# First feed-forward layer over two chunks at once: products of 256 columns in a Strassen-like scheme, with both chunks' state chains in one window

## The chip, the cores and the metric

The kernel runs on one core of a Trainium2 chip. The metric is the device time of one execution in microseconds (us). A core has a matrix engine (TensorE, PE in the profile, with its weight loads shown as PEld), three engines for elementwise work (VectorE = DVE, ScalarE = ACT, GpSimd = POOL) and SyncE (SP), whose queue issues nearly all DMAs here. Each engine works through its own instructions in order; semaphores tie the engines together. Matrix products accumulate in PSUM, everything else lives in SBUF, 128 partitions wide.

## What is computed

Two blocks in a row, all in float32: a delta-rule attention over 4 batches, 8 heads, 768 steps, head size 48, and a feed-forward net with an exact GELU on its 3072 tokens of 384 values (hidden size 2048).

```python
k_n = k / (np.linalg.norm(k, axis=-1, keepdims=True) + 1e-06)
state = np.zeros((B, H, D, D))
for t in range(S):
    kt, vt, bt = k_n[:, :, t], v[:, :, t], beta[:, :, t, None]
    y[:, :, t] = np.einsum('bhd,bhde->bhe', q[:, :, t], state)
    v_old = np.einsum('bhde,bhd->bhe', state, kt)
    state = state + bt[..., None] * np.einsum('bhd,bhe->bhde', kt, vt - v_old)
x = y.transpose(0, 2, 1, 3).reshape(B * S, H * D)
h = x @ w_in
out = (0.5 * h * (1.0 + erf(h / sqrt(2)))) @ w_out
```

The weights come as 64-bit floats and are decoded on the chip in the first part of the run.

## The kernel before

**Tiling.** The 768 steps are cut into 12 chunks of 64. A chunk has two tiles (`Unit`, u.a = 0, 1), each with two batches on the 128 partitions, so a chunk is 256 tokens for the feed-forward net. Two chunks make a group (32 tile-heads, four tiles).

**State chain of a chunk.** `against_state` multiplies the state by the keys and the queries (K products, L667, 64 matmuls); `subtract` forms W = (K product - V) times a factor on DVE (L678, L684) and copies y on ACT (L679); `solve` multiplies W by the group's inverse (L702), and ACT copies the result U (L710, L712); `use` forms the chunk's outputs and the state's increment (L732, L743); `next_state` (L748) and `read` (L758) add them on DVE; `turns` transposes the outputs x on PE (L788), and ACT copies them to xT. Only then the feed-forward net can begin on this chunk. The next chunk's chain needs the new state.

**What a group needs beforehand.** Keys and queries are loaded by DMA into block layouts (`load_blocks`, L138, eight DMAs a tile) and transposed on DVE (`turned_k` L399 into Kt, six buffers; `turned_q` L404 into Qt). `grams` (L414) multiplies keys by keys, `queries` (L414, then L450 on DVE) queries by keys, giving P. `norms` and `prep` square the keys on ACT, reduce on DVE (L349) and raise to a power on POOL (L351); `finish` (L303 to L307 on DVE) makes the factors; `scale_v` multiplies V by the norms on POOL (L376). The elimination (`eliminate_steps`) inverts 32 x 32 triangles on DVE, all of a group's at once: `scales` (L476, then the product of the mask `low` with the factors, L477, into XM), `flip` (a transpose, L482), `scaled_flip` (L487), 28 rows of two operations each (L501 writes tmp, L503 adds it to Nu) and two more L496, the diagonal L507, and transposes back into XM (L512) and Zf (L516). `join_run` then joins the 32 x 32 blocks to 64 x 64 (J1, J2: PE L593, DVE L605, ACT L572 into Zf).

**Feed-forward net.** Chunks 0 and 1 run it plainly (`fc1` L811, products of 256 columns; `fc2` L829, 384 columns). From chunk 2 on, both layers use a Strassen-like scheme with 7 instead of 8 products. In the first layer `mix_x` (L884) makes the input sums on DVE; then for each block of hidden features come eleven groups of matmuls in the order P1 P5 P6 P2 R22 R11 P7 P3 R12 P4 R21 (`part_of_layer`, L916). The two operands that the scheme combines are the chunk's two tiles, so a product has 128 columns. A chunk has NB = 2 blocks with FB = 4 matmuls in each group, 88 matmuls. DVE adds partial sums (L939 after P6, `add_p5` L968, L947 after P7, L958 after P4), and ACT copies and applies GELU into G (L902). P7, P4 and R21 add to the accumulator that L939 and L968 have worked on, P4 and R21 after L947 has read it. In the second layer `mix` makes the sums of G (L976, L977, L979, L981), seven products of eight matmuls with 192 columns follow (`second_layer`, L859), and `read2` (L1010 to L1021) puts the output together.

**Order.** A plan of (time, step) pairs is sorted and emitted; one unit of time is one chunk of the feed-forward net, and FFN(c) fills the unit from c+1 to c+2. DVE executes its steps exactly in the emitted order. PE runs in `together` blocks tied to the line of feed-forward products (`behind`). The chain of chunk c stands in FFN(c-1). The elimination of a group is given times from -0.35 to 1.167 around an odd unit (`rows_of`), so its rows lie over some one and a half units. So DVE has its rows, the sums of both layers and the chain's small operations in one order, and a step that waits holds up everything behind it on DVE.

Of the kernel before, what the change touches and what calls it, by code (L numbers as in the profile page):

```python
# [19 lines left out]
def kernel(  # L20
# [28 lines left out]
    nc = tc.nc  # L49
# [120 lines left out]
    low = cpool.tile([128, HB, HB], F32)  # L170
# [11 lines left out]
    G = cpool.tile([128, NA, NF, 128], F32)  # L182
# [126 lines left out]
    def squares(u, n, engine=None):  # L309
        kd = u.Kn[:, :, 0:D]  # L310
        if engine is nc.gpsimd:
            ksq = su.tile([128, H, D], F32, tag="w_e", name="ksq")
        else:
            ksq = wk.tile([128, H, D], F32, tag="x", name="ksq")
        if engine is None:
            keep(nc.scalar.activation, ksq, kd, ACT.Square)
            u.ksq = ksq
            return
        engine.tensor_tensor(ksq, kd, kd, op=ALU.mult)
        nc.vector.tensor_reduce(n, ksq, axis=AX.X, op=ALU.add)  # L320

    def sum_of_squares(u, h):

        if "both" not in ns:
            n23 = wk.tile([128, 2 * NA, H], F32, tag="n23", name="n23", bufs=1)
            ns[2], ns[3] = n23[:, 0:NA], n23[:, NA:]
            ns["both"] = n23
        if h == 0:
            u.ksq = wk.tile([128, H, D], F32, tag="ksq", name="ksq", bufs=1)
        keep(nc.scalar.activation, u.ksq[:, h], u.Kn[:, h, 0:D], ACT.Square,  # L330
             accum_out=ns[u.c][:, u.a, h:h + 1])
# [138 lines left out]
    def eliminate_steps(g):  # L470
        steps = []

        def scales():
# [3 lines left out]
            (nc.vector if g > 1 else nc.gpsimd).tensor_tensor(gl, low, gt.unsqueeze(2).to_broadcast([128, HB, HB]),  # L477
                                    op=ALU.mult)
# [172 lines left out]
    def against_state(us):  # L651

        for u in us:
            u.W = wk.tile([128, H, D], F32, tag="W", name="W")
# [53 lines left out]
    def solved(u, copy):  # L708
        u.U = wk.tile([128, H, D], F32, tag="U", name="U")
# [40 lines left out]
    def read(u, copy=nc.scalar.copy):  # L750
        u.x = wk.tile([128, H, D], F32, tag="x", name="x")
# [13 lines left out]

    def turn(u):
        if u.a == 0:
            xTs[u.c] = wk.tile([128, NM, NA * 128], F32, tag="xT", name="xT")
# [13 lines left out]
    def turns(us):  # L782
        c = us[0].c
        xT = xTs[c] = wk.tile([128, NM, NA * 128], F32, tag="xT", name="xT")
# [66 lines left out]
    A = [[G[:, a, k * FH:(k + 1) * FH] for k in range(2)] for a in range(NA)]  # L851
# [10 lines left out]
    FB = FH // 2  # L862
    NB = FH // FB
    S1, L1 = {}, {}

# [10 lines left out]
    def of_x(c, k, a):  # L876
        return xTs[c][:, k, a * 128:(a + 1) * 128]

    def mix_x(c):
        t = more[0].tile([128, 3, 128], F32, tag="TX", name="TX")  # L880
# [25 lines left out]
    def part_of_layer(c, b, n):  # L906

        fs = slice(b * FB, (b + 1) * FB)
# [11 lines left out]
        def half(k, a):  # L920
            return A[a][k][:, fs]

        def fresh(name, tag, pool):
            L1[name] = pool.tile([128, FB, 128], F32, tag=tag, name=f"ps{name}")
            return L1[name]

        if n == "P1":
            if b == 0:
                L1["pu"] = more[0].tile([128, 2, FB, 128], F32, tag="S1", name="pu")
# [12 lines left out]
        elif n == "R11":  # L942
            product(L1["X1"], block(0, 2), of_x(c, 2, 0), False)
            keep(nc.scalar.activation, half(0, 0), L1["X1"], ACT.Gelu)
        elif n == "P7":
            product(L1["Y1"], S1[3], L1["T"][3], False)
            nc.vector.tensor_tensor(half(1, 1), L1["Y1"], L1["pu"][:, 0], op=ALU.add)  # L947
# [8 lines left out]
        elif n == "P4":  # L956
            product(L1["Y1"], block(1, 1), L1["T"][4], False)
            nc.vector.tensor_tensor(half(0, 1), L1["V1"], L1["pu"][:, 1], op=ALU.add)  # L958
        else:
            product(L1["Y1"], block(1, 2), of_x(c, 2, 0), False)  # L960
            keep(nc.scalar.activation, half(1, 0), L1["Y1"], ACT.Gelu)
# [8 lines left out]
    def mix(c, n, h):  # L970
        fs = slice(h * FH // 2, (h + 1) * FH // 2)
        a11, a12, a21, a22 = (A[a][k][:, fs] for a in range(2) for k in range(2))
        if n == 1:
            if h == 0:
                W2["S"] = L1["pu"].rearrange("q e f n -> q (e f) n")
# [7 lines left out]
    def two(c, n):  # L983
        if n == 1:
# [56 lines left out]
    def ffn_steps(c):  # L1041
        ones = [(1.3, fc1, c, f) for f in range(NF)]
        if c > 1:
            return [(0.88, part_of_layer, c, b, n) for b in range(NB)
                    for n in ("P1", "P5", "P6", "P2", "R22", "R11", "P7", "P3", "R12", "P4", "R21")] + [
                (2.6, second_layer, c, n) for n in (1, 5, 2, 6, 4, 7, 3)]
# [131 lines left out]
    def late():  # L1178
# [3 lines left out]
        for a in range(NA):  # L1182
            Kb = more[0].tile([128, 2, NP, 2, HB], F32, name=f"Kb{a}")
            nc.scalar.mul(Kb.rearrange("q p j h n -> q (p j h n)"),
                          low.rearrange("q a b -> q (a b)")[:, 0:NP * 4 * HB], 0.0)
            for c in range(5, NC, 2):
                tiles[c, a].Kb = Kb
# [8 lines left out]
    plan = [at(c + 1 + 0.25 * (c == 1), c + 2 + 0.25 * (c == 0), ffn_steps(c)) for c in range(NC)]  # L1196
# [25 lines left out]
    plan += [at(c + 0.958, c + 0.959, [(1.0, mix_x, c)]) for c in range(2, NC)]  # L1222
    plan += [at(c - 0.4, c - 0.3, v_steps(c)) for c in range(4, NC)]
    plan += [at(2.08, 2.44, [(1.0, scale_head, tiles[c, a], h)
                             for c in (2, 3) for a in range(NA) for h in range(H)])]
    plan += [at(c - 1.0, c - 0.99, [(1.0, load_v, c)]) for c in range(3, NC)]
    for c in range(4, NC):
        us = [tiles[c, a] for a in range(NA)]
        t = {4: 1.8, 5: 2.1, 6: 3.25}.get(c, c - 2.9)
        plan += [at(t, t + 0.01, [(1.0, load_blocks, c, "Kb", k)])]  # L1230
        t = 3.2 if c == 4 else c - (0.72 if c % 2 == 0 else 0.9)
        plan += [at(t, t + 0.01, [(1.0, load_blocks, c, "Qb", q)])]
        t = c - (2.1 if c % 2 == 0 else 2.62) if c > 5 else {4: 2.1, 5: 2.74}[c]
        plan += [at(t, t + 0.01, [(1.0, load_k, c, "Kn")])]
        plan += [at(c - 0.4, c - 0.39, [(1.0, load_k, c, "Kp")])]
        t = {4: 2.7262, 5: 2.955}.get(c, c - (1.77 if c % 2 == 0 else 2.57))
        plan += [at(t, t + 0.0005, [(1.0, turned_k, u) for u in us])]
        t = c + (-0.12 if c % 2 == 0 else 0.23)
# [19 lines left out]
    for c in range(2, NC):  # L1258
        for b in range(NB):
            t = c + 1.06 + 0.2576 * b  # L1260
            plan += [at(t, t + 0.001, [(1.0, add_p5)])]
        plan += [at(c + 1.42, c + 1.421, [(1.0, mix, c, 1, 0)]),
                 at(c + 1.94, c + 1.941, [(1.0, read_x, c)]),
                 at(c + 1.715, c + 1.716, [(1.0, mix, c, 3, h) for h in range(2)])]
    for w in range(3, NC):
        two_ahead = w + 2 < NC
        if w % 2:
            if w == 3:
                plan += [at(w + 0.19, w + 0.191, [(1.0, transposed, u, (1,)) for u in fourth]),
                         at(w + 0.1, w + 0.101, [(1.0, together, *gram(5))]),  # L1270
                         at(w - 0.07, w - 0.069, [(1.0, norms, 5)]), at(w - 0.039, w - 0.038, [(1.0, prep, 5)]),
                         at(w + 0.11, w + 0.111, [(1.0, finish, 4)])]
                plan += rows_of(2, w, ((1, 0.112, 0.113), (2, 0.16, 0.2), (4, 0.224, 0.31),
                                       (2, 0.325, 0.365), (1, 0.395, 0.4), (2, 0.485, 0.5),
                                       (2, 0.508, 0.54), (5, 0.6, 0.685), (7, 0.76, 0.88),
                                       (3, 1.0, 1.05), (5, 1.07, 1.1), (1, 1.153, 1.154),
                                       (1, 1.2, 1.201), (1, 1.201, 1.202)))
            elif two_ahead:
                plan += rows_of(w // 2 + 1, w, ((1, -0.35, -0.349), (1, -0.34, -0.339),
                                                (1, -0.23, -0.229), (5, -0.22, -0.14),  # L1280
                                                (1, -0.07, -0.06), (3, 0.005, 0.05),
                                                (3, 0.068, 0.148), (2, 0.156, 0.215),
                                                (2, 0.235, 0.31), (3, 0.325, 0.365),
                                                (1, 0.398, 0.409), (2, 0.485, 0.5),
                                                (1, 0.508, 0.54), (5, 0.6, 0.685),
                                                (3, 0.76, 0.8), (1, 1.003, 1.004),
                                                (1, 1.16, 1.161), (1, 1.166, 1.167)))
            plan += [state_at(w, w + 0.367, w + 0.59, w + 0.72, w + 0.93, second=query(w))]
        else:
            j0, j1, j2 = join_steps(w // 2)  # L1290
            t = w + (0.25 if w == 4 else 0.165)
            plan += [at(t, t + 0.001, [(1.0, together, j0, *query(w))]),
                     at(w + 0.37, w + 0.371, [(1.0, together, j1, *gram(w + 2))]),
                     state_at(w, w + 0.465, w + 0.58, w + 0.72, w + 0.93, second=[j2] + gram(w + 3))]
            plan += spread("join", 4, w + 0.395)
            plan += spread("join", 4, w + 0.64)
            if two_ahead:
                plan += spread("gram", 2, w + 0.375) + spread("gram", 2, w + 0.42)
                plan += spread("gram", 4, w + 0.63)
                plan += [at(w + 0.366, w + 0.367, [(1.0, norms, w + 2)]), at(w + 0.3715, w + 0.372, [(1.0, prep, w + 2)]),  # L1300
                         at(w + 0.56, w + 0.561, [(1.0, norms, w + 3), (1.0, prep, w + 3)]),
# [33 lines left out]
```

## Time and profile before

| | |
|---|---|
| median of three runs | 640.89 us (640.38 to 640.94) |
| span of the profiled execution, first to last instruction | 638.7 us |
| mean granted TensorE clock | 0.985 |
| ACT busy | 259.9 us (41%) |
| POOL busy | 64.9 us (10%) |
| first-layer products, psX | 480 matmuls, 64.5 us |
| second-layer products, psX | 320 matmuls, 55.3 us |

Each float32 matmul is carried out in two recorded passes, and the recorded length of one holds its pipeline's tail: the pitch from one start to the next is what a matmul costs. By slices of a fortieth of the span (16 us), the digits are tenths of busy time; PEclk is the granted clock:

```profile
PE   6779999999999999999999999999999999999997
DVE  6999989999799987999677999577999565354342
POOL 4044002100300012001012001012001000000000
PEclk9977999999999999999999999999999999999999
```

After the first two or three slices PE has hardly any idle time. DVE alternates, and its last quarter is light, since no elimination is left. From 214 us on the chunks have a regular period of 45 to 46 us.

### The profile page before, as it was taken

How to read it: one execution, taken by the hardware profiler on the slowest of the kernel's cores; microseconds unless marked ns; L12 is line 12 of the kernel's file. 1: busy time of each engine (PE TensorE's matmuls, PEld its weight loads, DVE VectorE, ACT ScalarE, POOL GpSimd, SP SyncE). 2: the span in 40 equal slices, each digit the busy share in tenths (PEclk: the TensorE clock that was granted, in tenths of full speed). 3: DMA queues.
4: the chain of work that ended last, by engine and by line, in shares of the span. 5: the costliest groups of instructions: out<-in, count | busy, mean ns of one | idle time of the engine just before them, and what ended most of it. 6: DMA issues, size and time to landing. Idle time of an engine off the chain costs nothing.

```text
span 638.7 us, 22156 instructions
## 1 busy us (share of the span) xinstructions
PE 618.4 (97%) x9702; PEld 573.8 (90%) x9702; DVE 496.6 (78%) x1011; ACT 259.9 (41%) x586; POOL 64.9 (10%) x58
## 2 busy tenths in 40 slices
PE   6779999999999999999999999999999999999997
PEld 5667776776899999999999999999999999999997
DVE  6999989999799987999677999577999565354342
ACT  3576877624541265132265132265142253231230
POOL 4044002100300012001012001012001000000000
PEclk9977999999999999999999999999999999999999
DMA  9794884303442234221335222311222300100101
GB/s 134 172 280 139 149 175 137 50 1 73 73 67 44 47 51 77 56 36 36 58 48 79 54 27 47 57 27 28 52 29 38 62 4 2 26 2 3 26 2 25
DMA packets 158433, 39.79 MB, mean 62 GB/s; under 512 B 150016, under 2 KB 153216, under 8 KB 158336
## 3 DMA queue, kind: packets, MB, share of 16 engines
q1 hardware_dynamic: 155664, 37.34, 30.2%
q8 instruction: 76, 1.25, 0.8%
q10 hardware_dynamic: 2672, 1.03, 0.8%
q14 instruction: 21, 0.17, 0.1%
HBM read 33.62 MB, written 4.72 MB: 60 GB/s over the span
## 4 chain that ended last, share of the span: by engine, by line
PE 81%; DVE 11%; ACT 2%; DMA 2%; issue 2%; POOL 0%; SPq 0%; DVEq 0%; ACTq 0%; POOLq 0%
PE psX L859 12%; PE psY L916 11%; PE psX L916 8%; PE psY L859 8%; PE psV L916 5%; PE psZ L916 5%; PE psG L414 5%; PE psZ L859 4%; PE psV L859 4%; PE psK L667 3%; PE psO L829 3%; PE psJ L593 2%; DVE tmp L501 2%; DVE Nu L503 2%; PE psH L811 2%; PE psY L732 2%
## 5 line engine op out<-in xcount | busy, mean ns | idle before, releaser
L916 PE MATMUL psX<-xT,w_in_sb 128*128 128x128 f32 x480 | 64.5, 277 | 0.0
L503 DVE TENSOR_TENSOR Nu<-Nu,tmp 128x58 f32<-128x58 f32 (+13 forms) x168 | 58.5, 348 | 5.8
L501 DVE TENSOR_TENSOR tmp<-Nu 128x58 f32<-128x58 f32 (+13 forms) x168 | 59.2, 352 | 4.4
L916 PEld LDWEIGHTS psX<-xT,w_in_sb 128*128 128x128 f32 x480 | 58.8, 192 | 1.2 <-issue 0.3
L902 ACT COPY xT<-psX 128x768 f32<-128x768 f32 x9 | 7.2, 799 | 124.3 <-PE psX L788 124.3
L351 POOL TENSOR_TENSOR n<-n,half 128x16 f32<-128x16 f32 x10 | 30.2, 3020 | 247.2 <-DVE n L349 197.4
L859 PE MATMUL psX<-w_out_sb,G 128*128 128x192 f32 x320 | 55.3, 326 | 0.0
L859 PEld LDWEIGHTS psX<-w_out_sb,G 128*128 128x128 f32 x320 | 52.1, 190 | 0.0
L811 PE MATMUL psH<-xT,w_in_sb 128*128 128x256 f32 x192 | 44.4, 384 | 1.5 <-ACT G L902 1.3
L829 PE MATMUL psO<-w_out_sb,G 128*128 128x384 f32 x128 | 43.9, 490 | 0.0
L811 PEld LDWEIGHTS psH<-xT,w_in_sb 128*128 128x128 f32 x192 | 35.7, 190 | 8.8 <-ACT G L902 2.2
L916 PE MATMUL psY<-xT,w_in_sb 128*128 128x128 f32 x320 | 42.3, 275 | 0.0
L902 ACT COPY pu<-psZ 128x512 f32<-128x512 f32 x40 | 23.5, 587 | 39.5 <-PE psZ L916 39.5
L916 PEld LDWEIGHTS psY<-xT,w_in_sb 128*128 128x128 f32 x320 | 38.9, 192 | 0.0
L829 PEld LDWEIGHTS psO<-w_out_sb,G 128*128 128x128 f32 x128 | 23.6, 190 | 14.0
L902 ACT ACTIVATE G<-G 128x512 f32<-128x512 f32 x40 | 25.2, 629 | 20.5 <-DVE G L947 19.8
L376 POOL TENSOR_TENSOR V<-V,n 128x384 f32<-128x384 f32 x18 | 17.2, 965 | 135.3 <-DMA V<-in_v_dram 131.1
L939 DVE TENSOR_TENSOR psY<-psY,pu 128x512 f32<-128x512 f32 x20 | 14.0, 699 | 20.5 <-PE psY L916 18.7
L859 PE MATMUL psZ<-T,pu 128*128 128x192 f32 x160 | 28.6, 332 | 0.0
L859 PE MATMUL psY<-T,G 128*128 128x192 f32 x160 | 28.6, 332 | 0.0
L859 PE MATMUL psV<-w_out_sb,G 128*128 128x192 f32 x160 | 27.7, 326 | 0.0
L859 PE MATMUL psX<-T,G 128*128 128x192 f32 x160 | 27.6, 326 | 0.0
(183 smaller groups left out, 1349.7 us busy)
## 6 DMA issues: line engine op xcount, KB each, us to landing
Kp<-in_k_dram SPq DMA_DIRECT2D x76, 96.0 KB, 3.1
w_out_sb<-in_moe_w_in_dram SPq DMA_DIRECT2D x24, 256.0 KB, 4.1
w_raw<-in_moe_w_out_dram SPq DMA_DIRECT2D x16, 384.0 KB, 4.8
V<-in_v_dram SPq DMA_DIRECT2D x48, 96.0 KB, 3.1
out_dram<-o_sb SPq DMA_DIRECT2D x40, 96.0 KB, 2.2
Qp<-in_q_dram SPq DMA_DIRECT2D x64, 32.0 KB, 2.1
Qp<-in_q_dram SPq DMA_DIRECT2D x16, 96.0 KB, 4.4
Qp<-in_k_dram SPq DMA_DIRECT2D x32, 32.0 KB, 2.2
```

The lines of the kernel that those rows point to most:

```text
L351: nc.gpsimd.tensor_tensor(flat, flat, half, op=ALU.pow)
L376: engine.tensor_tensor(u.V, u.V, ns[u.c][:, u.a].unsqueeze(2).to_broadcast([128, H, D]), op=ALU.mult)
L414: nc.tensor.matmul(psG[HALF[p], r, i * NP + j, :], lhsT=u.Kt[rows, p, j, :], rhs=(u.Qt if x else u.Kt)[rows, p, j, :], start=True, stop=True)
L501: nc.vector.tensor_tensor(tmp, nu[:, j + 1:, j:j + 1].to_broadcast([128, n, j]), nu[:, j:j + 1, 0:j].to_broadcast([128, n, j]), op=ALU.mult)
L503: nc.vector.tensor_tensor(nu[:, j + 1:, 0:j], nu[:, j + 1:, 0:j], tmp, op=ALU.add)
L667: nc.tensor.matmul(u.psK[to, x, r, j, :], lhsT=(u.Qt if x else u.Kt)[rows, p, j, :], rhs=St[rows, u.a, p ^ r, j, :], start=True, stop=True)
L811: nc.tensor.matmul(psH, lhsT=w_in_sb[:, f // 2, m, f % 2 * 128:(f % 2 + 1) * 128], rhs=xTs[c][:, m, :], start=(m == 0), stop=(m == NM - 1))
L829: nc.tensor.matmul(u.psO, lhsT=G[:, u.a, f, :], rhs=w_out_sb[:, f, :], start=(f == 0), stop=(f == NF - 1))
L859: nc.tensor.matmul(ps_, lhsT=lhs[:, f, :], rhs=rhs[:, f, :], start=first and f == 0, stop=f == FH - 1, skip_group_check=not first)
L902: i = fn(*args, **kw)
L916: nc.tensor.matmul(ps_[:, i], lhsT=lhs[:, f // 2, f % 2 * 128:(f % 2 + 1) * 128], rhs=rhs, start=first and i == 0, stop=True, skip_group_c ...
L939: nc.vector.tensor_tensor(L1["Y1"], L1["Y1"], L1["pu"][:, 0], op=ALU.add)
```

## The change

From chunk 4 on the first layer runs over pairs of chunks (4,5), (6,7), (8,9), (10,11). The operands that the scheme combines are now the two whole chunks, so a product has 256 columns; a pair has four blocks with two matmuls in each group, 88 matmuls a pair. After a pair's first layer the second layers of both its chunks follow, unchanged. For that:

- G is there twice, xT holds a pair, and both state chains of a pair run in the window before: chunk 4's and 5's in FFN(3), chunk 6's and 7's in the second layers of pair (4,5), and so on.
- To make room, V, W, U and x of a tile share one buffer (a new V is loaded after `turns` has read x), `low` and the early squares live in the second G until it is used, the two extra tiles for odd chunks' key blocks are gone (all chunks use the same two), and the key squares use the tile of `mix_x`.
- From group 1 on XM is made by an `affine_select` on POOL instead of a product with `low` (on DVE for groups 2 to 5).
- All rows of the elimination for groups 3, 4, 5 stand in the first layer of the pair before, up to the join; group 2's stay where they were.
- Loads, transposes, norms and V's scaling get new times. Among them the transposes L399 for chunk 6 go from 4.23 to 3.5, into FFN(2), those for chunk 7 stay at 4.43, and those for later chunks go from c-1.77 and c-2.57 to c-2.5 and c-2.92.

```diff
@@ scales
-            (nc.vector if g > 1 else nc.gpsimd).tensor_tensor(gl, low, gt.unsqueeze(2).to_broadcast([128, HB, HB]),
-                                    op=ALU.mult)
+            wide = gt.unsqueeze(2).to_broadcast([128, HB, HB])
+            if g == 0:
+                nc.gpsimd.tensor_tensor(gl, low, wide, op=ALU.mult)
+            else:
+                nc.gpsimd.affine_select(out=gl, in_=wide, compare_op=ALU.is_ge, fill=0.0, base=-1,
+                                        pattern=[[1, HB], [-1, HB]], channel_multiplier=0)
@@ against_state, solved, read
-            u.W = wk.tile([128, H, D], F32, tag="W", name="W")
+            u.W = u.V
...
-        u.U = wk.tile([128, H, D], F32, tag="U", name="U")
+        u.U = u.W
...
-        u.x = wk.tile([128, H, D], F32, tag="x", name="x")
+        u.x = u.U if u.c else wk.tile([128, H, D], F32, tag="y", name="x")
@@ turns, of_g, blocks, of_x, part_of_layer
+    def new_tokens(c):
+        if c % 2 == 0:
+            xTs["pair", c] = wk.tile([128, NM, 2, NA * 128], F32, tag="xT", name="xT", bufs=1)
+        xTs[c] = xTs["pair", c - c % 2][:, :, c % 2]
...
+    def of_g(c):
+        g = Gp[c % 2 if c > 3 else 0]
+        return [[g[:, a, k * FH:(k + 1) * FH] for k in range(2)] for a in range(NA)]
...
+    def blocks(c):
+        return FH // 2 if c < 4 else FH // 4
...
     def of_x(c, k, a):
+        if c > 3:
+            return xTs[c + a][:, k]
         return xTs[c][:, k, a * 128:(a + 1) * 128]
...
+        FB = blocks(c)
+        NB = FH // FB
+        n_ = 512 // FB
...
-            L1[name] = pool.tile([128, FB, 128], F32, tag=tag, name=f"ps{name}")
+            L1[name] = pool.tile([128, FB, n_], F32, tag=tag, name=f"ps{name}")
@@ ffn_steps
-                (2.6, second_layer, c, n) for n in (1, 5, 2, 6, 4, 7, 3)]
+                (2.6, second_layer, cc, n) for cc in range(c, c + 1 + (c > 3))
+                for n in (1, 5, 2, 6, 4, 7, 3)]
@@ late
-        for a in range(NA):
-            Kb = more[0].tile([128, 2, NP, 2, HB], F32, name=f"Kb{a}")
...
-            for c in range(5, NC, 2):
-                tiles[c, a].Kb = Kb
@@ plan
-    plan += [at(c - 0.4, c - 0.3, v_steps(c)) for c in range(4, NC)]
+    plan += [at(t, t + 0.1, v_steps(c)) for c in range(4, NC)
+             for t in (4.3 if c == 5 else c - (0.4 if c % 2 == 0 else 0.85),)]
...
-        t = {4: 1.8, 5: 2.1, 6: 3.25}.get(c, c - 2.9)
-        plan += [at(t, t + 0.01, [(1.0, load_blocks, c, "Kb", k)])]
...
+        for name, src, t in (("Kb", k, {4: 1.8, 5: 2.73, 6: 3.25}.get(c, c - (2.8 if even else 3.45))),
+                             ("Qb", q, {4: 3.2, 5: 3.9}.get(c, c - (1.2 if even else 1.24)))):
+            plan += [at(t, t + 0.01, [(1.0, load_blocks, c, name, src)])]
...
-        t = {4: 2.7262, 5: 2.955}.get(c, c - (1.77 if c % 2 == 0 else 2.57))
+        t = {4: 2.7262, 5: 2.955, 7: 4.43}.get(c, c - (2.5 if even else 2.92))
         plan += [at(t, t + 0.0005, [(1.0, turned_k, u) for u in us])]
...
+    for w in range(4, NC, 2):
+        more_to_come = w + 2 < NC
+        if w == 4:
+            begins = 0.25, 0.33, 0.41, 0.51, 0.6, 0.66, 0.7, 0.78, 0.87, 0.945
+            n6, p6, n7, p7 = 0.53, 0.56, 0.75, 0.8
+        else:
+            begins = -0.22, -0.1, 0.02, 0.14, 0.27, 0.38, 0.42, 0.6, 0.76, 0.93
+            n6, p6, n7, p7 = 0.3, 0.34, 0.56, 0.58
+            plan += rows_of(w // 2, w, ((1, *((-1.19, -1.189) if w > 6 else (-1.05, -1.049))),
+                                        (1, *((-1.18, -1.179) if w > 6 else (-1.04, -1.039))),
+                                        (1, -1.035, -1.034), (4, -1.03, -1.0),
+                                        (3, -1.0, -0.95), (3, -0.935, -0.855), (2, -0.843, -0.785), (1, -0.77, -0.75),
+                                        (3, -0.742, -0.692), (3, -0.677, -0.597), (2, -0.585, -0.527), (1, -0.512, -0.5),
+                                        (3, -0.484, -0.434), (3, -0.419, -0.339), (2, -0.327, -0.269),
+                                        (2, -0.255, -0.245), (2, -0.24, -0.23)))
+        begins = [w + t for t in begins]
+        j0, j1, j2 = join_steps(w // 2)
+        plan += [at(begins[0], begins[0] + 0.001, [(1.0, together, j0, *query(w))]),
+                 at(begins[1], begins[1] + 0.001, [(1.0, together, j1, *gram(w + 2))]),
+                 state_at(w, *begins[2:6], second=[j2] + gram(w + 3)),
+                 state_at(w + 1, *begins[6:], second=query(w + 1))]
...
+            plan += [at(w + n6, w + n6 + 0.001, [(1.0, norms, w + 2)]), at(w + p6, w + p6 + 0.001, [(1.0, prep, w + 2)]),
+                     at(w + n7, w + n7 + 0.001, [(1.0, norms, w + 3)]), at(w + p7, w + p7 + 0.001, [(1.0, prep, w + 3)]),
+                     at(w + p7 + 0.04, w + p7 + 0.041, [(1.0, finish, w + 2)])]
```

The program then has 4570 instead of 4922 matmuls, 794 instead of 814 two-tensor operations on DVE, nine instead of four selects on POOL, and 485 DMAs issued by SP as before.

## The prediction

> **What bounds the kernel now.** I read the page's busy shares first, then its groups, then windows cut where a stage begins, and last TensorE's and VectorE's timelines instruction by instruction. Busy shares and groups:
>
> ```profile
> PE 618.4 (97%) x9702; PEld 573.8 (90%) x9702; DVE 496.6 (78%) x1011; ACT 259.9 (41%) x586; POOL 64.9 (10%) x58
> L916 PE MATMUL psX<-xT,w_in_sb 128*128 128x128 f32 x480 | 64.5, 277 | 0.0
> L503 DVE TENSOR_TENSOR Nu<-Nu,tmp 128x58 f32<-128x58 f32 (+13 forms) x168 | 58.5, 348 | 5.8
> L501 DVE TENSOR_TENSOR tmp<-Nu 128x58 f32<-128x58 f32 (+13 forms) x168 | 59.2, 352 | 4.4
> ```
>
> TensorE is the limit, at 97%. But DVE at 78% is an average; windows (columns: the window, its length, PE, PEld, DVE, ACT, POOL busy, granted clock, DMA share, GB/s) show what it hides:
>
> ```profile
> 46.00:54.00 8.00, 6.43 (x180) 5.80 (x178) 7.90 (x9) 6.58 (x18) 6.21 (x7) 0.50 0.12 18
> 402.00:448.00 46.00, 46.00 (x905) 44.60 (x904) 32.71 (x55) 23.68 (x47) 7.42 (x4) 1.00 0.21 37
> 448.00:494.00 46.00, 46.00 (x685) 45.23 (x684) 43.41 (x105) 12.30 (x25) 2.12 (x2) 1.00 0.22 37
> ```
>
> PE fills both 46 us units of the last two rows (one chunk of the feed-forward net each), so PE work sets the end. DVE has 13.3 us spare in one unit and 2.6 in the next, the one with most of an elimination. A change that packs this DVE work tighter can hand the bound to DVE.
>
> **The gain: wider first-layer products.** Starts of neighbouring groups in TensorE's timeline give the pitch (two recorded passes per fp32 matmul; the lengths hold a pipeline tail):
>
> ```profile
> 76.88 5.45 PE L811 MATMUL psH<-xT,w_in_sb 128*128 128x256 f32 x24
> 83.34 2.86 PE L811 MATMUL psH<-xT,w_in_sb 128*128 128x256 f32 x12
> ...
> 216.85 1.06 PE L916 MATMUL psX<-xT,w_in_sb 128*128 128x128 f32 x8
> 217.75 1.06 PE L916 MATMUL psZ<-xT,w_in_sb 128*128 128x128 f32 x8
> ```
>
> 128 columns: (217.75-216.85)/8 = 0.112 us a pass. 256 columns: (5.45-2.86)/12 = 0.2157. Chunks 4 to 11 have 8 x 88 = 704 matmuls, 157.7 us; as four pairs 352, 151.9. Gain 5.85 us. mix_x runs 4 times less and an XM product leaves DVE, but what decides below is where DVE's work stands. (The Trainium skill, "TensorE: Matmul & The Clock Gate", section "Wait — 56ns, not 53.3ns?", puts the fixed cost of a warm matmul at about 2.5 ns: 704 passes fewer would save 1.8 us, and the sum would end 4.1 higher. The trace has 2 x 112 - 215.7 = 8 ns per pair of passes; I keep the row.)
>
> **Loss 1, start of FFN(2).** Kt of chunk 5 now goes through the same buffer as chunk 4's, and its two transposes (0.63 us each) and chunk 5's two reduces (0.46 each) stand on DVE ahead of mix_x. The squares they read end on ACT at 164.67. So 164.67+0.05+0.46+1.26+0.32 = 166.77 for mix_x's first result, and product P5 starts near 166.9 instead of 165.98: +0.9.
>
> **Loss 2, rest of FFN(2).** Two transposes L399 (chunk 6's Kt) move ahead of L976 there. Kt has six buffers, so they wait for chunk 3's queries (L414):
>
> ```profile
> 192.30 0.68 DVE L976 TENSOR_TENSOR pu<-G 128x512 f32<-128x512 f32 x1
> ...
> 213.47 0.32 DVE L1013 TENSOR_TENSOR p<-psY,p 128x192 f32<-128x192 f32 x1
> ```
> ```profile
> 194.13 1.13 PE L414 MATMUL psG<-Qt,Kt 48*64 48x64 f32 x64
> ...
> 213.94 1.13 PE L916 MATMUL psX<-xT,w_in_sb 128*128 128x128 f32 x8
> ```
>
> From 192.30 to 213.86 DVE is never idle, and FFN(3)'s first product at 213.94 takes the accumulator that L1013 has just read. The queries' first half ends at about 194.70; DVE starts at 194.85, spends 1.26 on the transposes and reaches L976 at 196.11: 3.81 late, with nothing after it to absorb that. +3.8. Below: 0 if the loads and buffers let them run earlier, which the six-buffer count excludes.
>
> **Loss 3, FFN(3).** Both chains of chunks 4 and 5 now run here. A join waits for L958 (+0.4), the second use for ACT's gram copies (+0.65); I add both, bounds 0 and 1.05. Then chunk 7's norm is put on DVE between P of chunk 5 and its state and x:
>
> ```profile
> 245.26 1.01 DVE L349 TENSOR_REDUCE n<-ksq 128x8 f32<-128x384 f32 x2
> 249.28 0.18 DVE L303 TENSOR_SCALAR n<-n 128x32 f32<-128x32 f32 x1 [3.01 <-POOL n L351]
> ```
>
> DVE stands still while POOL takes the power. After the queries DVE needs 0.15 + P 1.135 + reduces 0.93 + POOL 2.90 and 0.1 of handoff + L303 to L307 1.95 + St and x of both tiles 3.16 = 10.3. PE has two groups of the second layer (2.7 each) and `use` (2.0), 7.4, before turns reads x. +2.9. Sum of this window 3.95.
>
> **Loss 4, the pairs.** An elimination used to run over some 1.5 units. Now all its rows stand in the first layer of the pair before, and join J1 (L593), which reads their result XM, follows the 33rd product. PE gets there 33 x 4 x 0.2157 + 0.43 = 28.9 us after the pair's first product. What DVE must issue before: mix_x 1.45 (0.93 now at 128 columns), L482 1.93, the last read of the second layer (L1021) 0.28, L487 1.25, 56 row operations and two L496 21.5, L507 0.13, three blocks of L939+L968+L947+L958 at 0.80+0.61+0.66+0.60 = 2.67, 8.0; L399 twice 1.26; L512 2.05. Sum 37.85. The 21.5 are start-to-start distances, 0.26 to 0.44 by row length:
>
> ```profile
> 216.18 0.33 DVE L503 TENSOR_TENSOR Nu<-Nu,tmp 128x168 f32<-128x168 f32 x1
> 216.55 0.32 DVE L501 TENSOR_TENSOR tmp<-Nu 128x150 f32<-128x150 f32 x1
> ...
> 217.79 0.69 DVE L939 TENSOR_TENSOR psY<-psY,pu 128x512 f32<-128x512 f32 x1
> 218.59 0.69 DVE L968 TENSOR_TENSOR pu<-psY,pu 128x512 f32<-128x512 f32 x1
> ...
> 221.64 2.10 DVE L512 STREAM_TRANSPOSE XM<-Nu 128x1024 f32<-128x1024 f32 x1
> ```
>
> Pair (4,5): DVE starts 1.5 ahead of the first product; 36.35-28.9 = 7.45 of PE waiting, about half of it already in block 0, where P7 needs L968 and L968 stands behind 13 row operations. Pair (6,7): the flip L482 is done earlier, the rest runs from L1021, that is from PE's last second-layer group: 34.65-28.9 = 5.75. Pair (8,9): no L399 in between, 4.5. Pair (10,11) eliminates nothing: 0. Together +17.7. After J1 DVE has no rows left, and the second layers, with both chains of the next chunks, come to no more than 0.2 of new waiting. The SP queue (485 DMAs before and after) and the loads moved on it come to nothing: they are issued at least a unit ahead, and a late V load would show first in POOL's scaling, next.
>
> **POOL beside DVE.** V is scaled in the same first layers now, twice a pair, and the mask product of XM goes from DVE to POOL. Before, a scaling slowed the row operation beside it:
>
> ```profile
> 189.66 0.83 POOL L376 TENSOR_TENSOR V<-V,n 128x384 f32<-128x384 f32 x1 [15.32 <-DMA V<-in_v_dram]
> 189.83 0.86 DVE L501 TENSOR_TENSOR tmp<-Nu 128x184 f32<-128x184 f32 x1
> ```
>
> 0.86 against 0.35 for that form: +0.5 each, two a pair in three pairs, 3.1. The new select on POOL (not in this trace; 1.27 for the nearest, L173, to 1.91 for POOL's L477) lies beside L482, which ran at 1.95 beside POOL, and for the first pair beside mix_x: +0.5. Bounds 0 and 3.65; I take 3.65, since the rows are the same pair of operations.
>
> **Sum.** -5.85 + 0.9 + 3.8 + 3.95 + 17.7 + 3.65 = +24.15. The profiled span of 638.7 would be 662.9; with the 2.2 us that separate it from the median of 640.89, 665.0.
>
> **Rivals.**
> A, other side: DVE's work stays hidden and the gain stands alone: 640.9-5.85 = 635.0. For it: DVE is busy 78%, and 13.3 us are free in every second unit. Against: the rows are not spread over those units any more. It decides if DVE got through its 37.85 in 28.9 us, 24% faster than its own rows run now.
> B: only the pairs stall; the tiles of FFN(2) and FFN(3) come in time: 640.9-5.85+17.7 = 652.8, up to 656.4 with POOL. For it: those waits hang on the exact order around one buffer. Against: DVE had no idle moment in FFN(2).
> C: the waits bring the clock down. The first window above had PE at 80% busy and a clock of 0.50. Against, the page's other row: later waits of 1.3 to 1.7 us
>
> ```profile
> 58.00:66.00 8.00, 6.70 (x89) 5.15 (x88) 7.58 (x12) 4.63 (x7) 0.00 (x0) 1.00 0.82 236
> ```
>
> left it at 1.00. My three longest waits (3.8, 2.9 and 3.7) lie in between. If each costs half of an 8 us window at 0.50, 4 us, the time is 665+12 = 677. (The same page of the skill, section "What's actually happening", has the gate close after an idle window of about 3.4 us and reopen after as much work; two such windows at half clock would add 3.4, giving 668.4.)
> D: the wider products don't come about: excluded by the order of instructions, which has 352 matmuls less.
>
> **Chances.** Forecast 0.62, A 0.08, B 0.15, C 0.13, the rest 0.02. The forecast's own range is 661 (no POOL contention) to 669; the full range, 652 to 677, takes in B and C and leaves A out. A measurement tells about 0.2%, 1.3 us. Faster 0.09, same 0.02, slower 0.89.
>
> **What would show it.** L916 groups of 128x256 at 0.216 us a pass. In the first layers of pairs (4,5), (6,7), (8,9): DVE busy throughout, PE waiting before psY products on DVE, and before L593 on L512, the latter product starting 33 to 36 us after the pair's first. In FFN(3): L788 waiting on x. FFN(3)'s first L916 waiting on L1013. Clock 1.00 in the pairs, unless C. I am wrong if PE stays at its 99% there, if row operations run at pitches under 0.30, or if loads end these waits instead of DVE.

## The result and the profile after

| | before | after |
|---|---|---|
| median | 640.69 us (640.38 to 640.94, 4 runs) | 671.77 us (669.02 to 675.23, 4 runs) |
| ratio | | 1.0488, 95% interval 1.0454 to 1.0522 |
| profiled span | 638.7 us | 669.5 us |
| granted clock, mean | 0.985 | 0.962 |
| DVE busy | 496.6 us | 490.1 us |

Slower by 31 us, forecast 665.0 within 652 to 677. The changed kernel has its own line numbers: first-layer products are L943 (L916 before), add_p5 L1002 (L968), the other additions L971, L979, L991 (L939, L947, L958), rows L510 and L512 (L501, L503), the flip's scaling L496 (L487), the transposes into XM and Zf L521 and L525 (L512, L516), join products L602 (L593), turns L803 (L788), V's scaling L381 (L376), the helper of ScalarE's kept copies L926 (L902).

The page's busy shares, and two neighbouring groups of TensorE's timeline in a pair:

```profile
PE 621.9 (93%) x8998; PEld 551.8 (82%) x8998; DVE 490.1 (73%) x991; ACT 258.6 (39%) x584; POOL 68.1 (10%) x62
```
```profile
284.68 1.03 PE L943 MATMUL psY<-TX,Sw 128*128 128x256 f32 x4
285.54 1.03 PE L943 MATMUL psX<-xT,w_in_sb 128*128 128x256 f32 x4
```

Over all such neighbours the median distance is 0.863 us for four passes (0.2158 a pass), and in the kernel before 0.893 us for eight of 128 columns (0.1116 a pass). So the gain is 704 x 2 x 0.1116 - 352 x 2 x 0.2158 = 5.2 us, a little under the forecast. DVE is not busier than before, and TensorE at 93% waits more. What it waits for (columns: engine and tile, what ended the wait, us in total, times, longest), leaving out the first part of the run, which is 0.6 us shorter than before (FFN(2)'s first product starts at 164.48 instead of 165.09):

```profile
PE psY L943 <- DVE pu L1002: 10.9, 5, 5.1
...
PE psJ L602 <- DVE XM L521: 3.2, 4, 0.9
PE psX L943 <- ACT pu L926: 3.2, 3, 1.1
...
PE psX L803 <- DVE V L767: 2.3, 2, 1.2
...
PE psY L877 <- DVE o_sb L1045: 2.0, 1, 2.0
PE psZ L943 <- DVE TX L908: 1.7, 1, 1.7
...
PE psX L943 <- DVE p L1048: 1.2, 1, 1.2
PE psV L877 <- ACT y L688: 1.1, 3, 0.4
```

The heaviest wait is P7's for add_p5. TensorE's and VectorE's timelines at the beginning of pair (4,5) show how it comes about:

```profile
287.27 1.03 PE L943 MATMUL psX<-xT,w_in_sb 128*128 128x256 f32 x4
293.39 2.08 PE L943 MATMUL psY<-xT,w_in_sb 128*128 128x256 f32 x4 [5.10 <-DVE pu L1002]
295.26 1.91 PE L943 MATMUL psV<-xT,Sw 128*128 128x256 f32 x4
...
321.15 1.15 PE L602 MATMUL psJ<-XM,G 32*64 32x64 f32 x32 [0.87 <-DVE XM L521]
```
```profile
291.60 0.33 DVE L512 TENSOR_TENSOR Nu<-Nu,tmp 128x168 f32<-128x168 f32 x1
291.85 0.69 DVE L971 TENSOR_TENSOR psY<-psY,pu 128x512 f32<-128x512 f32 x1
292.65 0.69 DVE L1002 TENSOR_TENSOR pu<-psY,pu 128x512 f32<-128x512 f32 x1
```

DVE comes to L971 without a pause, 6 us after PE had finished P6, the sum that L971 adds to (at 285.7), because the flip and its scaling and 13 row operations stand ahead. After the wait the groups are 1.87 and 1.71 apart instead of 0.86, half the clock. The join starts 38.20 us after the pair's first product (282.95), and 34.79 and 34.83 in the next two pairs.

To place the whole loss I took every group of matmuls from FFN(2) on and subtracted passes times pitch from the distance to the next group's start (for the small groups, their shortest distance in the same run). That excess is 11.6 us before and 48.1 after: +36.5. With the gain of 5.2 that makes +31.3, which is what the stretch from FFN(2)'s first product to the last group has grown by (466.7 to 498.0). The spans differ by 30.9, because the first part is 0.6 shorter. The account has to close by the way it is made; what it adds is the place of each loss.

### The profile page after: what moved, and what is told of

Same layout as the page of the kernel before. It is cut to its first block, busy times and chain, and to the rows that moved or that the text cites. A ratio compares the mean times of both kernels' runs of the same rounds, so it can differ in the third digit from the quotient of the medians.

```text
span 669.5 us, 20804 instructions
## 1 busy us (share of the span) xinstructions
PE 621.9 (93%) x8998; PEld 551.8 (82%) x8998; DVE 490.1 (73%) x991; ACT 258.6 (39%) x584; POOL 68.1 (10%) x62
## 4 chain that ended last, share of the span: by engine, by line
PE 62%; DVE 25%; issue 6%; ACT 3%; DMA 1%; POOL 1%; SPq 0%; DVEq 0%; ACTq 0%; POOLq 0%
PE psX L877 10%; PE psY L943 8%; PE psY L877 7%; PE psX L943 5%; PE psV L943 4%; DVE tmp L510 4%; DVE Nu L512 4%; PE psG L419 4%; PE psV L877 3%; PE psZ L877 3%; PE psZ L943 3%; PE psO L844 2%; PE psK L676 2%; PE psH L826 2%; PE psT L398 2%
## 5 line engine op out<-in xcount | busy, mean ns | idle before, releaser
L943 PE MATMUL psX<-xT,w_in_sb 128*128 128x256 f32 (+1 forms) x288 | 63.7, 349 | 4.4 <-ACT pu L926 3.2
L512 DVE TENSOR_TENSOR Nu<-Nu,tmp 128x58 f32<-128x58 f32 (+13 forms) x168 | 59.0, 351 | 5.8
L510 DVE TENSOR_TENSOR tmp<-Nu 128x58 f32<-128x58 f32 (+13 forms) x168 | 56.9, 339 | 4.6
L943 PEld LDWEIGHTS psX<-xT,w_in_sb 128*128 128x128 f32 x288 | 47.4, 191 | 11.0 <-ACT pu L926 4.4
L943 PE MATMUL psY<-xT,w_in_sb 128*128 128x256 f32 (+1 forms) x192 | 44.2, 361 | 10.9 <-DVE pu L1002 10.9
L943 PEld LDWEIGHTS psY<-xT,w_in_sb 128*128 128x128 f32 x192 | 32.7, 196 | 16.2 <-DVE pu L1002 12.9
L926 ACT COPY pu<-psZ 128x512 f32<-128x512 f32 x40 | 23.5, 586 | 45.2 <-PE psZ L943 23.2
L926 ACT COPY xT<-psX 128x768 f32<-128x768 f32 x9 | 7.2, 799 | 85.3 <-PE psX L803 85.3
L926 ACT ACTIVATE G<-G 128x512 f32<-128x512 f32 x40 | 25.2, 630 | 26.9 <-DVE G L979 26.5
L1015 DVE TENSOR_TENSOR G<-G 128x512 f32<-128x512 f32 x20 | 13.6, 690 | 25.7 <-PE psX L877 25.7
L877 PE MATMUL psY<-w_out_sb,G 128*128 128x192 f32 x160 | 27.9, 327 | 2.0 <-DVE o_sb L1045 2.0
```

The costliest lines, as they stand in the source:

```text
L510: nc.vector.tensor_tensor(tmp, nu[:, j + 1:, j:j + 1].to_broadcast([128, n, j]), nu[:, j:j + 1, 0:j].to_broadcast([128, n, j]), op=ALU.mult)
L512: nc.vector.tensor_tensor(nu[:, j + 1:, 0:j], nu[:, j + 1:, 0:j], tmp, op=ALU.add)
L877: nc.tensor.matmul(ps_, lhsT=lhs[:, f, :], rhs=rhs[:, f, :], start=first and f == 0, stop=f == FH - 1, skip_group_check=not first)
L926: i = fn(*args, **kw)
L943: nc.tensor.matmul(ps_[:, i], lhsT=lhs[:, f // 2, f % 2 * 128:(f % 2 + 1) * 128], rhs=rhs, start=first and i == 0, stop=True, skip_group_c ...
L1015: nc.vector.tensor_tensor(a12, a12, a11, op=ALU.subtract)
```

## The experiments

Each is an edit of the changed kernel; medians are beside 639.8 to 640.3 us for the kernel before on the same chips. FFN(2) is the same in the changed kernel and in experiments 1, 3 to 6, 10 and 11, yet it took 56.07 and 56.03 us in the profiles of the changed kernel and of 11 and 54.05 to 54.92 in the other six, and the first part of the run varies by 1.6. So a difference of two microseconds between medians says little, and what an edit does is read from the stretch that it touches.

**1. No rows.** `eliminate` returns at once for groups 3 to 5:

```diff
+            if g > 2:
+                return
             nu = Nus[g]
```

> The changed kernel without the row operations (L501, L503, L496 of before) of groups 3, 4 and 5; the inverse of these groups is then not formed. My theory: VectorE's chain up to the join sets the pairs, so the waits of block 0 (5.3, 2.6, 3.1 us), the half clock after them (2.5, 1.8, 1.8) and the small ones up to the join (1.4, 1.4, 1.0) all go: 671.8 - 20.9 = 651. ScalarE's waits after the join (1.2 each) stay, the early ones too. Rival, loads or POOL or the clock hold the pairs and VectorE only shows it: not under 665.

Measured 655.57 us (653.30 to 660.43), ratio to before 1.0253 (1.0209 to 1.0297): 16.2 less, not 20.9. The join comes after 31.35, 29.97 and 29.97 us. In the two later pairs nothing is left of the waits in block 0 (1.3 in the first), and no half clock. So the rows make the waits, not loads. The join's own wait, which I had counted among those to go, stayed. TensorE and VectorE there, without any rows:

```profile
311.30 0.59 PE L945 MATMUL psX<-xT,w_in_sb 128*128 128x256 f32 x2
312.78 0.62 PE L604 MATMUL psJ<-XM,G 32*64 32x64 f32 x14 [0.88 <-DVE XM L523]
```
```profile
309.78 0.69 DVE L993 TENSOR_TENSOR G<-psV,pu 128x512 f32<-128x512 f32 x1 [0.96 <-PE psV L945]
310.45 0.09 DVE L518 MEMSET Nu<- 128x32 f32 x1
310.57 2.07 DVE L523 STREAM_TRANSPOSE XM<-Nu 128x1024 f32<-128x1024 f32 x1
```

(Here L993 is the addition L991, and L523 the transpose L521.) DVE has been idle, but the transpose stands behind an addition that PE feeds two and a half products before the join. From the addition's start at 309.78 DVE needs 0.7 + 0.1 + 2.1 us; PE needs 1.95, since its last half product, from 311.30, takes 0.43. The order alone costs 1.05 us a pair.

**2. The early windows put right.** Chunk 5's keys and squares earlier, chunk 5's and 6's key transposes later (and chunk 7's key blocks loaded later), the factors of chunks 6 and 7 after chunk 5's outputs:

```diff
-at(2.93, 2.931, [(1.0, norms, 5)])
+at(2.89, 2.891, [(1.0, norms, 5)])
...
-{4: 2.7262, 5: 2.955, 7: 4.43}.get(c, ...)
+{4: 2.7262, 5: 2.9592, 6: 4.0, 7: 4.43}.get(c, ...)
-at(w + p7 + 0.04, ..., [(1.0, finish, w + 2)])
+at(w + (0.92 if w == 4 else p7 + 0.04), ..., [(1.0, finish, w + 2)])
```

> The changed kernel with the early windows put right: chunk 5's squares earlier, chunk 5's and 6's key transposes later, the factors of chunks 6 and 7 after chunk 5's outputs. My theory: these orders cost 7.4 us in FFN(2) (1.65 of it half clock) and 2.8 in FFN(3); 671.8 - 10 = 662, with FFN(2) back near 49 us from first product to first product (56.1 now, 48.9 before) and the waits of the turns in FFN(3) gone. Rival: they are hidden behind the pairs, which VectorE sets anyway, and the time stays at 672 within 2.

Measured 667.13 us (666.40 to 668.28), 4.6 less, not 10. FFN(2) takes 48.92 us from first product to first product, 48.84 before and 56.07 in the changed kernel: that loss is the order of three steps, as the theory has it. FFN(3) fell by 1.6 (62.39 to 60.80), but the wait of block 0 in pair (4,5) grew from 5.3 to 7.1 and its join came after 40.10. The factors (L306 to L310, 272.98 to 274.94) now stood directly ahead of mix_x on DVE, which began 0.3 us after the pair's first product and not 1.2 ahead of it. For this part the rival was right: the loss was handed on to a stretch that DVE sets. (Pair (8,9), which the edit doesn't touch, also took 1.4 more, with the clock at half for 6.8 us instead of 3.4.)

**3. TensorE kept warm.** Matmuls with unread results in the three long waits:

```diff
+            if b == 0 and 3 < c < 10:
+                psF = dn("psF")[:, 0, 0:256]
...
+                behind(warm, {4: 11, 6: 5, 8: 6}[c])
```

> The changed kernel with 11, 5 and 6 extra matmuls of 256 columns (4.7, 2.2 and 2.6 us, results unread) in the three long waits of block 0, so that TensorE doesn't stand still. My theory: the half clock after these waits (6.1 us in all) lies inside a stretch whose end, the join, VectorE sets; the time stays within 1.5 us of 671.8, though the clock is 1.00 in the pairs. Rival: the clock costs what it shows, and the time falls by 6 to 665.7.

Measured 670.33 us (669.02 to 671.17). The same stretch, first product to join, in the changed kernel and here (columns: the window, its length, busy of PE, PEld, DVE, ACT, POOL, granted clock, DMA share, GB/s):

```profile
282.95:321.15 38.20, 31.98 (x136) 26.81 (x135) 35.03 (x81) 11.67 (x20) 1.66 (x2) 0.91 0.25 43
```
```profile
283.46:320.86 37.40, 34.98 (x158) 29.07 (x157) 35.33 (x81) 11.62 (x20) 2.76 (x2) 1.00 0.25 42
```

The clock is whole and the stretch only 0.8 shorter (0.2 and 0.65 in the other pairs, of 2.5, 1.8 and 1.8 lost to the clock). A slow clock inside a stretch that another engine sets costs what it delays that engine, here DVE's wait for psV (0.81 us at L991 in the changed kernel), and not what the matmuls lose.

**4. Rows dealt out evenly.** Three instead of seven rows ahead of the first add_p5:

```diff
-(4, -1.03, -1.0), (3, -1.0, -0.95), (3, -0.935, -0.855), (2, -0.843, -0.785), (1, -0.77, -0.75),
+(3, -1.03, -1.0), (4, -0.935, -0.855), (3, -0.843, -0.785), (1, -0.77, -0.75),
...
```

> The changed kernel with the 30 rows of groups 3 to 5 dealt out differently over the four blocks: 3 instead of 7 ahead of the first add_p5, the others later. My theory: the sum of VectorE's work up to the join decides, not the place of one wait: the wait in block 0 falls from 5.3 to about 2.6 us in pair (4,5) and goes in the others, later waits grow, and the join stands where it stood (38.2, 34.8 and 34.9 us after the pair's first product); 671.8 within 2. Rival: the 13 operations ahead of add_p5 are what costs; then 8 to 14 us less.

Measured 668.42 us (668.30 to 672.56), 3.35 less: more than the 2 that I had allowed, far from the rival's 8. The joins come after 37.29, 34.09 and 33.71, 0.7 to 1.1 earlier. P7's wait in pair (4,5) fell to 2.5, and new ones of 0.9 and 1.4 came in blocks 1 and 2. DVE now ran without a pause from mix_x to the join in that pair. So the sum decides, and the place of a wait moves the join by a microsecond.

**5. Join and copies later.** J1 two products later, the copies of Zf on ScalarE after those of P1 and P5:

```diff
-(2, -0.255, -0.245), (2, -0.24, -0.23)
+(2, -0.255, -0.245), (1, -0.24, -0.235), (1, -0.14, -0.139)
-begins = -0.22, -0.1, ...
+begins = -0.175, -0.1, ...
```

> The changed kernel with join J1 two products later in the last block (after P1 and P5 of it) and ScalarE's copies of Zf after the copies of P1 and P5 there. My theory: J1's wait of 1.05 us was there without any row too, because the transpose into XM stands behind VectorE's last addition of block 2, which PE feeds 2 products earlier; and the 1.2 after it is ScalarE's copy of P1's sum behind two Zf copies of 1.05. Both go, 2.25 in three pairs: 665. Rival: the row operations set J1; then only the 1.2 go, 668.

Measured 664.53 us (662.12 to 665.36): both waits are gone in all three pairs. That the time meets the 665 so well is partly luck. By the profiles the pairs fell by 1.2, 2.3 and 2.8 us: in pair (4,5) block 0's wait grew by 0.5, in pair (8,9) part of the gain is a clock that stayed whole, and 2.0 more came from FFN(2), which the edit doesn't touch. The second wait is one that I had not seen coming at all. ScalarE's timeline in the changed kernel, in pair (4,5):

```profile
324.04 2.10 ACT L529 COPY Zf<-Zf 32x1024 f32<-32x1024 f32 x2 [3.56 <-DVE Zf L525]
326.16 0.58 ACT L926 COPY pu<-psX 128x512 f32<-128x512 f32 x1
```

P1's sum lay ready, but its copy stood behind two copies of Zf that waited for DVE's transpose; PE waited 1.2 us for the operand.

**6. Rows earlier.** Norms of the next chunks, flip, scaling and the first rows in DVE's gaps of FFN(3) and of the second layers:

```diff
-            n6, p6, n7, p7 = 0.3, 0.34, 0.56, 0.58
+            n6, p6, n7, p7 = 0.12, 0.2, 0.34, 0.4
-  (1, -1.18, -1.179), (1, -1.035, -1.034), (4, -1.03, -1.0), (3, -1.0, -0.95), ...
+  (1, -1.525, -1.524), (1, -1.395, -1.394), (3, -1.39, -1.38), (3, -1.28, -1.26), (4, -1.235, -1.2), (2, -1.03, -0.96), ...
...
```

> The changed kernel with the norms of the next two chunks earlier in the second layers, so that XM, the flip, its scaling and the first 4 (group 3) or 11 (groups 4, 5) rows run in VectorE's gaps there and in FFN(3), and fewer are left in the first layers. My theory: work of 4.2 and about 7.5 us leaves VectorE's chain; J1 comes 33.7 us after the first product in pair (4,5) and 30 in the others (30.0 with no rows at all), and the turns of FFN(3) don't wait for the norm: -4.5 - 4.8 - 4.8 - 2.8 = 655. Rival: VectorE's gaps in the second layers are where the chain needs it at once; the rows there make x or P late, the waits come back at turns and use, and it ends over 664.

Measured 655.19 us (654.84 to 655.50); joins after 34.31, 30.34 and 30.37, the turns of FFN(3) without a wait. By the profiles the pairs fell by 12.5 us (forecast 14.1) and FFN(3) by 2.65; another 1.4 is FFN(2)'s, which the edit doesn't touch. The same work in other gaps of the same engine: DVE is not short of time, it was short of time in that place.

**7. Everything together**, with the turns of a pair's first chunk after the K products of its second.

> Everything together: the early rows, the later join, the early windows' transposes put right, and the turns of a pair's first chunk after the K products of its second. My theory: the parts add, 671.8 - 17 (rows) - 7.4 (FFN(2)) - 5 (join) - 1.5 (0.5 in each pair, y's copy ahead of the second layer) = 641, the kernel before within 0.5%; what is left over 635 is waits of under 1 us. Rival: they overlap, each giving back what another took, and it ends between 648 and 655.

Measured 641.34 us (640.92 to 643.06), ratio to before 1.0030 (1.0018 to 1.0043). TensorE is busy for 615.5 us (96%), DVE for 489.1 (76%). The excess by the account above is 18.2 us against 11.6 before: 6.7 us of small waits, 2.9 of them in pair (4,5), still eat the gain of 5.2. That makes +1.5 from FFN(2)'s first product on; the first part is 0.65 shorter, and the spans differ by 0.8.

**8 and 9. Finer.** Two tries at those waits: chunk 6's key transposes after block 0's last addition and chunk 8's in FFN(3) (8); then FFN(3)'s first layer as in 7, chunk 7's keys ahead of chunk 8's blocks, V of even chunks later (9).

> The kernel with everything, its left-over waits taken one by one: chunk 6's key transposes after the last addition of block 0 in FFN(3) (0.75 us there), the transpose into Zf after the addition behind it (0.44), and in pair (4,5) the flip, the scaling and chunk 8's key transposes in FFN(3)'s gaps, and a row less ahead of mix_x (2.9 us of waits in that pair), in the other pairs a row less ahead of P4 (0.3 each). My theory: of the 7 us that TensorE still waits more than before, 4 go: 641.3 - 4 = 637.3, 0.4% under the kernel before. Rival: VectorE's chain in pair (4,5) is still too long, or the moved work makes FFN(3)'s chain late, and it stays at 640 to 642.

> The kernel with everything again, with FFN(3)'s first layer as it was there, the flip, scaling and transposes of the finer run in FFN(3)'s gaps but chunk 7's keys loaded ahead of chunk 8's blocks, and V of chunks 6, 8, 10 loaded and scaled after the last join of the pair. My theory: in pair (4,5) 2 of 3 us of waits go (1.1 of them were row operations beside POOL's scaling), 641.3 - 2 = 639.3, level with the kernel before. Rival: V comes late to the state chain, or FFN(3) pays again: 641 to 643.

Measured 643.24 (642.18 to 643.81) and 643.28 us (642.17 to 643.74): no better, and a little above even the rivals' ranges. In 8 the waits went (0.75 at the transposes) and came back as 1.44 and 0.83 elsewhere in FFN(3), which took 0.9 us longer; pair (4,5) gained 0.3. (Its profiled run is 2.0 longer than 7's, but 1.4 of that lies ahead of FFN(2), where the two don't differ.) In 9 four scalings of V instead of two fell into pair (4,5), four row operations took 0.90 to 0.92 us (two in 8 took 1.02 and 0.92), and its join came after 35.93 against 33.73 in 8.

**10 and 11. POOL beside DVE.** First V's loads and scalings of even chunks later, then no scaling for chunks 6 to 11:

```diff
-        return [(1.0, scale_v, tiles[c, a]) for a in range(NA)]
+        return [(1.0, scale_v, tiles[c, a]) for a in range(NA) if c < 6]
```

> The changed kernel with one thing moved: V of chunks 6, 8, 10 is loaded and scaled at the end of the pair before instead of in its first blocks. The trace of the changed kernel has row operations and the flip's scaling longer by 0.5 each beside POOL (0.5, 0.5 and 1.05 us a pair). My theory: VectorE's chain gets shorter by that, 671.8 - 2 = 669.8, and the row operations have one length. Rival: the slowed operations lie in slack, and nothing moves (within 0.7).

> The changed kernel without POOL's scaling of V for chunks 6 to 11 (V enters unscaled), since moving its loads left it in the first layers. My theory: VectorE's row operations and the flip's scaling beside it lose their extra 0.5 each (0.5, 0.5 and 1.05 us in the three pairs by the trace of the changed kernel), J1 comes that much earlier (37.7, 34.3 and 33.8 us after the first product), 669.8. Rival: the slowed operations are hidden in slack, J1 stays at 38.2, 34.8 and 34.8.

Run 10 tells nothing of it: 671.15 us (670.62 to 673.07), and two scalings still stood in pair (4,5)'s first block, at 285.91 and 291.95: the last two V tiles can only be loaded when `turns` has read x of chunk 5, and SP issued these loads at 281.96 and 287.62 (282.23 and 287.55 in the changed kernel). Run 11 gave 668.23 us (665.55 to 670.94), joins after 38.44, 33.54 and 33.01: 1.25 and 1.8 earlier in two pairs, not earlier in the first. Part of these two gains is the clock, which stayed whole after waits of 2.05 us. POOL's effect on a single operation is plain in the changed kernel's timelines:

```profile
285.94 0.83 POOL L381 TENSOR_TENSOR V<-V,n 128x384 f32<-128x384 f32 x1 [3.25 <-PE psY L943]
```
```profile
286.10 1.74 DVE L496 TENSOR_TENSOR Nu<-Nu,XM 128x1024 f32<-128x1024 f32 x1
```

L496 takes 1.22 alone. Yet L971, which met the next scaling (at 291.82), took its usual 0.69; one of its operands is in PSUM. The Trainium skill, "SBUF — State Buffer", section "Who interferes with whom", has the rule: a VectorE operation with two inputs in SBUF contends with a GpSimd operation that reads SBUF; one with at most one, outside the modes that use both ports, doesn't. These rows agree. What it costs a whole pair stays between 0 and 1.8 us.

## Why the prediction was right, and where it was not

The measured 671.8 lies above the forecast's own 661 to 669; it is inside the full range because that takes in rival C, which accounts for 3.4 us at the most.

- **What bounds the kernel.** Right, with a wrong cut: the chunks before take 45.2 and 51.1 us by turns, not 45 to 46 each. Cut there (361.90 to 407.09, 407.09 to 458.20), DVE has 6.3 and 10.9 us to spare, not 2.6 and 13.3.
- **The gain, -5.85.** Right in kind, 0.6 too large: one distance of 0.90 us, read to two decimals, stood for 0.893. The wide products save 7.4 ns for each pair of passes, so the row was a better guide than the 2.5 ns quoted beside it.
- **Loss 1, +0.9.** Mis-sized: P5 started at 167.26 instead of 165.98 (the second reduce began at 165.27, the forecast had 164.72, and FFN(2)'s first product started 0.6 earlier). This wait of 1.7 us put the clock at half, which the step hadn't: the window from 168.35 to 171.99 was granted 0.53. With it 3.6 us.
- **Loss 2, +3.8.** Right: 2.2 before the product that waits for L1045 and 1.3 before FFN(3)'s first, 3.5, and experiment 2 gave them back by moving the transposes.
- **Loss 3, +3.95.** Right in mechanism and size for the norm ahead of x (2.8 at the turns of chunk 5, forecast 2.9); the other 1.05 came to 0.6. But this loss and the next are not independent, as experiment 2 showed.
- **Loss 4 with POOL, +21.35.** The joins came 9.3, 5.9 and 5.9 us later than 28.9, 21.1 in sum. The mechanism held, but that the sum fits to 0.3 is partly luck: with a third of POOL's part each, the forecast has 8.7, 7.0 and 5.7. And 1.05 in each pair is the order of the transpose behind the last addition, not the rows' length: against experiment 1 the rows add 6.9, 4.8 and 4.9, 16.5 in sum. Of POOL's 3.65, the select cost the first mix_x 0.75 (forecast 0.5) and the trace has 2.0 of row operations and scaling for the forecast 3.1.
- **"No more than 0.2 of new waiting" after J1: wrong.** This step failed. It was 1.2 us in each pair behind the Zf copies on ScalarE and 0.5 where psV waits for ScalarE's copy of y, 5.3 in all (waits and restart). I had followed DVE's queue operation by operation and taken ScalarE's, at 41%, for free.
- **Rival A (hidden)** fell because of place, as argued: DVE's share even fell. **Rival B** fell with experiment 2's 48.92. **Rival C** was half right: half clock came after four waits, 7.7 us of matmul time in all, but at the most 1.7 of it counted in the pairs (experiment 3), and 1.65 in FFN(2). The row set against it holds one wait of 1.3 us and none of 1.7.

So the 6.8 us between 665.0 and 671.8 are mainly the two waits on ScalarE (5.3 for 0.2) and loss 1 (3.6 for 0.9, 1.65 of it clock). The gain adds 0.6; losses 2 to 4 and the shorter first part take back 1.7.

## What to carry to other kernels

When a change packs an in-order engine's work into one stretch, sum that engine's queue from the first operation that can start to the one that the next stage waits for, and compare it with the other engine's work up to the same point; a busy share over the whole run says nothing about it. Do the same for every engine that copies in that stretch, also one at 40%. Once the stretch has a bound, losses inside it hide each other, so they don't add until the bound is moved, and then they do: 31 us became 1.6 by moving steps, with none of them removed.

## What was not expected of the hardware

The length of a wait does not say whether the clock drops. Over its pitch, P5 in FFN(2) came 1.55 to 1.95 us late in experiments 1, 3, 4 and 6 and the clock stayed whole; 1.9 us at the same place in the changed kernel and in experiment 11 cost half of it for 3.4 us. Waits of 2.05 in two pairs of experiment 11 and of 3.2 in pair (8,9) of experiment 5 left it whole, and 2.6, 3.1 and 5.3 us in the changed kernel cost half of it for 3.4, 3.4 and 6.8 us.

What the profiles show is a fixed grid. In the changed kernel the clock is at half from 168.50 to 171.91, 291.38 to 298.21, 397.20 to 400.61 and 499.60 to 503.01, and the starts are 36, 31 and 30 times 3.413 us apart. Cut into windows of that length on its own grid from 75 us on, every profile of this case shows the same. After each of the 17 windows at full clock in which TensorE was busy 1.4 us or less, the clock fell; with 1.45 to 1.72 us busy it fell after two of seven; with more, once (experiment 6, 2.56 us, mostly small products). Experiment 3 at the wait for L1045 (columns as above; the window's own clock is the third number from the end):

```profile
210.18:213.59 3.41, 1.39 (x9) 1.10 (x8) 3.29 (x8) 0.00 (x0) 0.00 (x0) 1.00 0.29 52
213.59:217.00 3.41, 3.41 (x12) 3.41 (x12) 3.16 (x8) 0.00 (x0) 0.00 (x0) 0.50 0.02 5
```

Experiment 1 has the same wait (TensorE idle for 2.02 us in both), with 1.46 us busy in the window (208.28 to 211.69), and the clock stayed whole; the 3.2 us of experiment 5 fell into two windows with 2.12 and 1.66 busy. So, as far as these profiles show, a wait counts by how much of it falls into one window. The Trainium skill, "TensorE: Matmul & The Clock Gate", section "What's actually happening", has a free-running window of about 3.4 us, which agrees, and a clock that falls after an idle window; here a window busy for up to 1.4 us was enough.

Whether the wide scheme can beat the kernel before stays open: its best version here is 0.3% slower, with 6.7 us of waits that two tries moved and did not remove.
